# Attention and a squared-ReLU feed-forward on one core: q's difference and normalisation on VectorE, a square that reads PSUM, and other half steps for the attention units

## The chip, the cores and the metric

The kernel runs on one core of a Trainium2 chip. The metric is the device time of the execution in microseconds (us). Its engines are TensorE (PE in the profile; its weight loads PEld), VectorE (DVE), ScalarE (ACT), GpSimd (POOL) and SyncE (SP), which here issues nearly all DMAs. Matmul results go to banks of PSUM; everything else lies in SBUF.

## The reference

```python
def _attn_ref(q, k, v):                       # 8 batches, 8 heads, 576 rows, 64 columns
    q_s = np.exp(q - np.max(q, axis=-1, keepdims=True))
    q_s = q_s / (np.sum(q_s, axis=-1, keepdims=True) + 1e-09)
    k_s = np.exp(k - np.max(k, axis=2, keepdims=True))
    k_s = k_s / (np.sum(k_s, axis=2, keepdims=True) + 1e-09)
    kv = np.einsum('bhsd,bhse->bhde', k_s, v)
    return np.einsum('bhsd,bhde->bhse', q_s, kv)

def _moe_ref(x, w_in, w_out):                 # 4608 tokens, 512 -> 2048 -> 512
    r = np.maximum(x @ w_in, 0.0)
    return (r * r) @ w_out
```

The attention is linear: q is normalised along its 64 columns, k along its rows, and the result of all heads of a batch, 576 tokens of 512 columns, is the input x of the feed-forward part.

## The kernel before

**Blocks, steps and half steps.** A batch gives a block of 512 tokens; the 64 tokens left over of each batch are put by in DRAM (`x_left`) and make a ninth block at the end. For a block, the 2048 hidden columns are worked in 16 chunks, and one chunk is one step. Step n does on PE the hidden products H(n) (`ffn_h`: 12 matmuls of 128x512, L350 to L352) and then the output products of the step two before, O(n-2) (`ffn_out`: 12 matmuls, L379 to L381). Every float32 product is split into a high and a low part in PE's rounded format, so that three matmuls (high x high, high x low, low x high) replace one.

**Around a step.** ScalarE takes the relu of the bank (L356), VectorE squares it (L357), ScalarE casts the square to g_hi (L362), and VectorE subtracts to get g_lo (L367), which stands ahead of the next step's square in VectorE's queue. H writes two banks in turn, so H(n+2) writes the bank of H(n). g_hi and g_lo have two buffers each, so the cast of step n needs O(n-2) to be done with its buffer.

**Units in half steps.** While block b runs through the feed-forward part, the attention of block b+1 is prepared beside it. Heads go in pairs (two heads lie on the 128 partitions of one product), and two pairs make a couple, the first and the second pair; a block has two couples, the first couple and the second couple. The steady part has 24 pairs, numbered from 0, in 12 couples. Each pair's work is cut into units, small functions that issue a few instructions, and `UNIT_AT` gives for each unit the half step, relative to the couple's base, in which it is issued: the first number for the first pair, the second for the second pair. Half step 2n lies between H(n) with its square and O(n-2); half step 2n+1 lies behind O(n-2) and the cast to g_hi of step n. The bases are half steps 6 and 20 of a block's 32 (`COUPLE_AT`). The whole order is written by hand in this way: each engine works its instructions in the order of issue, and waits are by semaphore. What is issued in one half step follows the number of the pair and then the order of names in `UNIT_AT`.

**The units.** For k: `k_max` reduces over the rows that a partition holds, `k_bound` makes from that one bound for all rows (two transposes of 32x32 blocks, small copies and reductions, L228 to L241), `k_less` subtracts it (L246), `k_exp` is ScalarE's exponential (L249). For q: `q_max` (L253), `q_less`, the difference (L258, GpSimd), `q_exp` (L261), `q_sum` (L265, and a small addition on GpSimd, L266), `q_recip` (L269), `q_norm`, the product with the reciprocal (L273, GpSimd), `q_turn`, a transpose in blocks (L277), `q_out` and `q_back`, which write the result to DRAM and load it back turned (L283, L288) into the one tile qT. `q_split` splits qT into a high part (ScalarE, L301) and a low part (GpSimd, L302) for each head, in the tiles qs.

**The products.** At the couple's base, `kv` does the key-value products of both pairs (L338) and VectorE scales them to kf. `parts` splits kf into the one tile kvs (ScalarE L211 and L294, VectorE L212). `low` and `high` are the attention products: 320 columns and 256 columns for each of the two heads (L311), into the two banks that the attention has. Each is emptied by two copies on ScalarE (L313) and two additions on VectorE (L314); then ScalarE casts x_hi (L318) and GpSimd subtracts to get x_lo (L319). Since both write the same two banks, high must wait until the additions of low have read them. `low` also writes the left-over tokens to `x_left`.

**Loads.** `load_after` issues the loads for the pair two further on: q behind `q_less`, the first pair's k behind `k_less`, the second pair's k and all v one half step behind the couple's products `kv`. All go through SP's queue, in order, as do q's way through DRAM and the output's stores.

**The first phase** (blocks 0 and 1 of attention, all weights, and the feed-forward part of block 0) follows a list of its own, `FIRST`, and ends at about 134 us. Its square (L602) reads the relu's result and the bank.

Of the kernel before, what the change touches and what calls it, by code (L numbers as in the profile page):

```python
# [14 lines left out]
ALU = mybir.AluOpType  # L15
AX = mybir.AxisListType

P = 128
HALF = 64
LOW = 5  # L20
# [14 lines left out]


UNIT_AT = dict(
    k_max=(-13, -5), k_bound=(-11, -3), k_less=(-9, -2), k_exp=(-9, -1), q_max=(-13, -6), q_less=(-12, -6),
    q_exp=(-11, -5), q_sum=(-10, -4), q_recip=(-9, -3), q_norm=(-9, -3), q_turn=(-7, -1), q_out=(-7, -1),
    q_back=(-6, 1), q_split=(-2, 5), parts=(0, 5), low=(3, 7), high=(4, 8),  # L40
)


# [50 lines left out]
def attention_ffn_kernel(ctx: ExitStack, tc: tile.TileContext, q, k, v, w_in, w_out, out):  # L94
    nc = tc.nc

    B, H, S, D = q.shape
# [95 lines left out]
    def tiles(b, pr):  # L193
        i = pr if b == 0 else pr % NB
        return kt[i], qt[i], (v0 if b == 0 else vt)[i]

    def load_one(b, pr, n):
        for part in range(4 if n == 2 and b else 2):
            load_part(b, pr, n, part)
# [14 lines left out]
    def attention(b, pr):  # L214

        kk, qq, vv = tiles(b, pr)
        st = {}
# [8 lines left out]
        def k_bound():  # L226
            mt = attn_pool.tile([P, 4, BLK], F32, name="mt", bufs=1)
            nc.vector.transpose(mt, st["m"].rearrange("p h (e a) -> p (h e) a", a=BLK))  # L228
            m1 = attn_pool.tile([P, 4], F32, name="m1", bufs=1)
            nc.vector.tensor_reduce(m1, mt, axis=AX.X, op=ALU.max)  # L230
            m4 = attn_pool.tile([BLK, 4, 4], F32, name="m4", bufs=1)
            for g in range(4):
                nc.vector.tensor_copy(m4[:, g], m1[g * BLK : (g + 1) * BLK])
            m5 = attn_pool.tile([P, 4, 1], F32, name="m5", bufs=1)
            for g in range(4):
                nc.vector.tensor_reduce(
                    m5[g * BLK : (g + 1) * BLK, :, 0], m4.rearrange("p g c -> p c g"), axis=AX.X, op=ALU.max
                )
            mb = attn_pool.tile([P, 2, 1, D], F32, name="mb", bufs=1)
            nc.vector.tensor_copy(mt, m5.broadcast_to([P, 4, BLK]))  # L240
            nc.vector.transpose(mb.rearrange("p h o (e a) -> p (h o e) a", a=BLK), mt)  # L241
            st["mb"] = mb
# [12 lines left out]
        def q_less():  # L255
            qn = st["qn"] = attn_pool.tile([P, LOW, 2, D], F32, name="qn", tag="qn", bufs=1)
            qm = st["qm"].broadcast_to([P, 2, LOW, D])
            nc.gpsimd.tensor_tensor(qn.rearrange("p j h d -> p h j d"), qq, qm, op=ALU.subtract)  # L258

        def q_exp():  # L260
            nc.scalar.activation(st["qn"], st["qn"], AF.Exp)  # L261
# [1 line left out]
        def q_sum():  # L263
            qs = st["qs"] = attn_pool.tile([P, LOW * 2, 1], F32, name="qs")
            nc.vector.tensor_reduce(qs, st["qn"].rearrange("p j h d -> p (j h) d"), axis=AX.X, op=ALU.add)  # L265
            nc.gpsimd.tensor_scalar_add(qs, qs, 1e-9)  # L266

        def q_recip():
            nc.vector.reciprocal(st["qs"], st["qs"])  # L269

        def q_norm():
            qv = st["qn"].rearrange("p j h d -> p (j h) d")
            nc.gpsimd.tensor_tensor(qv, qv, st["qs"].broadcast_to([P, LOW * 2, D]), op=ALU.mult)  # L273

        def q_turn():
            tb = st["tb"] = w_pool.tile([P, 4, LOW, BLK], F32, name="tb", tag="raw", bufs=RAWB)
# [28 lines left out]
        def attn(g0, nj):  # L305
            xf = w_pool.tile([P, 2, 2, nj, BLK], F32, name="xf", tag="raw", bufs=RAWB)
            x, corr = xf[:, 0], xf[:, 1]
            ps = [bank(2 * nj * BLK).rearrange("p (g j a) -> p g j a", g=2, a=BLK) for h in range(2)]
            for h in range(2):
                qs = st["q"][h][:, g0 : g0 + 2, :nj].rearrange("p g j a -> p g (j a)")  # L310
                nc.tensor.matmul(ps[h].rearrange("p g j a -> p g (j a)"), kvs[:, h], qs, start=True, stop=True)  # L311
            for h in range(2):
                nc.scalar.copy(corr[half[h]], ps[h][HALF:])  # L313
                nc.vector.tensor_tensor(x[half[h]], ps[h][:HALF], corr[half[h]], op=ALU.add)  # L314
            xh, xl = (
                t[b % 2][:, pr].rearrange("p (j g a) -> p g j a", g=4, a=BLK)[:, g0 : g0 + 2] for t in (x_hi, x_lo)
            )
            nc.scalar.copy(xh, x[:, :, :HIGH])  # L318
            nc.gpsimd.tensor_tensor(xl, x[:, :, :HIGH], xh.bitcast(F32), op=ALU.subtract)  # L319
            if nj == LOW:  # L320
                dst = x_left[:, pr, b * LEFT : (b + 1) * LEFT].rearrange("p (g a) -> p g a", g=2)
                nc.sync.dma_start(dst, x[:, :, HIGH])

        st["v"] = vv
        st["units"] = dict(
            k_max=k_max, k_bound=k_bound, k_less=k_less, k_exp=k_exp, q_max=q_max, q_less=q_less, q_exp=q_exp,
            q_sum=q_sum, q_recip=q_recip, q_norm=q_norm, q_turn=q_turn, q_out=q_out, q_back=q_back, q_split=q_split,
            parts=parts, low=lambda: attn(0, LOW), high=lambda: attn(2, HIGH),
        )
        return st  # L330
# [23 lines left out]
    def relu_square(ps):  # L354
        r = work.tile([P, NT], F32, name="r")
        nc.scalar.activation(r, ps, AF.Relu)  # L356
        nc.vector.tensor_tensor(r, r, r, op=ALU.mult)  # L357
        return r

    def high_part(r):  # L360
# [9 lines left out]
    def ffn_h(blk, fc):  # L370
        ps = next_bank("h")
        for cc in range(NCC):
            h_part(ps, blk, fc, cc)
        return ps
# [256 lines left out]
    def open_late():  # L631
# [3 lines left out]
        x_lo.append(late.tile([P, NCC, NT], F32R, name="x_lo1"))  # L635

    steady = [attention(2 + i // NPAIR, i % NPAIR) for i in range((B - 2) * NPAIR)]
    with tc.manual_schedule():
        first_phase()
# [8 lines left out]
    def at(slot, *units):  # L648
        slots.setdefault(slot, []).extend(units)

    def load_after(i, n):
        if i + NB < len(steady):
            load_one(2 + (i + NB) // NPAIR, (i + NB) % NPAIR, n)

    for i, st in enumerate(steady):
        base = 2 * NFC * (1 + i // NPAIR) + COUPLE_AT[i % NPAIR // 2]
        if i % 2 == 0:
            at(base, lambda i=i: kv(steady[i : i + 2]))
        for name, when in UNIT_AT.items():
            if i or name in ("q_split", "parts", "low", "high"):  # L660
                at(base + when[i % 2], st["units"][name])
            if i and name == "q_less":
                at(base + when[i % 2], lambda i=i: load_after(i, 1))
            elif i and name == "k_less" and i % 2 == 0:
                at(base + when[0], lambda i=i: load_after(i, 0))
        if i % 2:
            for j, part in (i, 0), (i - 1, 2), (i, 2):
                at(base + 1, lambda j=j, part=part: load_after(j, part))
# [8 lines left out]
    with tc.manual_schedule():  # L677
        for n in range(NFC, len(steps) + LAG):
            if n < len(steps):
                h = ffn_h(*steps[n])  # L680
                if mid:
                    gs[n - 1] = low_part(*mid)
                r = relu_square(h)
# [45 lines left out]
```

## Time and profile before

| | us |
|---|---|
| median of 3 runs | 910.36 (907.1 to 910.5) |
| the profiled execution | 907.09 |
| its span, first to last instruction | 905.1 |
| mean granted TensorE clock | 0.991 |

| engine | busy, us | share of the span |
|---|---|---|
| PE | 867.1 | 96% |
| VectorE | 579.4 | 64% |
| ScalarE | 407.6 | 45% |
| GpSimd | 280.7 | 31% |

A row of the profile's timeline gives the start, the duration, the engine, the line, the operation, the tile written and the tiles read, the shape, and in brackets the idle time ahead of it with what ended it. A row that ends in x2 or x4 merges instructions that follow each other. Matmuls are pipelined: a matmul of 512 columns is shown with 0.39 us, but back to back one starts every 0.227 us. A group's row gives its busy time in us and the mean of one in ns.

### The profile page before, as it was taken

The numbers are of one execution on the slowest core, as the hardware profiler recorded it, in microseconds if no ns is written. First come the engines' busy times: TensorE is split into PE (matmuls) and PEld (weight loads), VectorE is DVE, ScalarE is ACT, GpSimd is POOL, SyncE is SP. The second block draws the span as 40 slices with busy tenths as digits, with TensorE's granted clock in tenths as the row PEclk, the third lists the DMA queues.
The fourth block names the chain that finished last, engine by engine and source line by source line (L and its number), as shares of the span: only waits on it lengthen the run. The fifth ranks groups of instructions, "written<-read, shape, count | busy, mean of one in ns | idle before, by whom it ended". The sixth has DMA issues, their size and how long they took to land.

```text
span 905.1 us, 12692 instructions
## 1 busy us (share of the span) xinstructions
PE 867.1 (96%) x4391; PEld 706.2 (78%) x4391; DVE 579.4 (64%) x1075; ACT 407.6 (45%) x793; POOL 280.7 (31%) x261
## 2 busy tenths in 40 slices
PE   7999998899999999899989999899989999999998
PEld 7787777787887878787878788787878888888886
DVE  7897768767778578757867687857776433223222
ACT  5997653544444444444453544443453432222222
POOL 4695723323334223333333333422342200000000
PEclk8999999999999999999999999999999999999999
DMA  9999633230332224121323133222411030002001
GB/s 239 302 312 251 161 78 85 67 91 22 102 83 72 56 80 120 57 72 42 104 69 89 39 102 83 58 70 59 120 37 34 3 93 1 1 1 47 0 1 47
DMA packets 99552, 75.82 MB, mean 84 GB/s; under 512 B 49056, under 2 KB 88736, under 8 KB 99488
## 3 DMA queue, kind: packets, MB, share of 16 engines
q1 hardware_dynamic: 98832, 74.32, 30.5%
q10 hardware_dynamic: 656, 0.69, 0.3%
q8 instruction: 35, 0.57, 0.3%
q14 instruction: 29, 0.24, 0.1%
HBM read 55.31 MB, written 19.66 MB: 83 GB/s over the span
## 4 chain that ended last, share of the span: by engine, by line
PE 71%; DVE 13%; ACT 5%; DMA 4%; SPq 3%; issue 3%; POOL 0%; ACTq 0%; DVEq 0%; POOLq 0%
PE o_ps L379 12%; PE o_ps L380 11%; PE o_ps L381 11%; PE bank L350 10%; PE bank L352 10%; PE bank L351 10%; DVE kvs L212 2%; DVE xf L314 2%; DVE r L357 2%; ACT qs L301 2%; PE bank L338 1%; DMA bounce<-tb 1%; PE bank L311 1%; DMA vt<-in_v_dram 1%; ACT g_hi L362 1%
## 5 line engine op out<-in xcount | busy, mean ns | idle before, releaser
L379 PE MATMUL o_ps<-wo,g_hi 128*128 128x512 f32 x576 | 228.7, 397 | 0.0
L380 PE MATMUL o_ps<-wo,g_hi 128*128 128x512 f32 x576 | 226.3, 393 | 0.2 <-POOL wo L585 0.2
L381 PE MATMUL o_ps<-wo,g_lo 128*128 128x512 f32 x576 | 226.2, 393 | 0.1
L350 PE MATMUL bank<-x_hi,wi 128*128 128x512 f32 x568 | 222.1, 391 | 0.0
L352 PE MATMUL bank<-x_hi,wi 128*128 128x512 f32 x568 | 221.6, 390 | 0.4 <-POOL wi L585 0.3
L351 PE MATMUL bank<-x_lo,wi 128*128 128x512 f32 x568 | 221.3, 390 | 0.0
L357 DVE TENSOR_TENSOR r<-r 128x512 f32<-128x512 f32 x128 | 107.7, 841 | 137.7 <-ACT r L356 137.6
L362 ACT CAST g_hi<-r 128x512 fp32r<-128x512 f32 x128 | 79.5, 621 | 156.2 <-PE o_ps L380 108.4
L356 ACT ACTIVATE r<-bank 128x512 f32<-128x512 f32 x128 | 76.3, 596 | 159.1 <-PE bank L352 158.2
L367 DVE TENSOR_TENSOR g_lo<-r,g_hi 128x512 fp32r<-128x512 f32 x128 | 98.5, 770 | 62.7 <-ACT g_hi L362 62.4
L381 PEld LDWEIGHTS o_ps<-wo,g_lo 128*128 128x128 f32 x576 | 109.2, 190 | 23.8 <-DVE g_lo L608 0.4
L380 PEld LDWEIGHTS o_ps<-wo,g_hi 128*128 128x128 f32 x576 | 109.5, 190 | 22.3 <-POOL wo L585 0.8
L379 PEld LDWEIGHTS o_ps<-wo,g_hi 128*128 128x128 f32 x576 | 109.5, 190 | 22.2
L352 PEld LDWEIGHTS bank<-x_hi,wi 128*128 128x128 f32 x568 | 106.7, 188 | 23.7 <-POOL wi L585 1.2
L351 PEld LDWEIGHTS bank<-x_lo,wi 128*128 128x128 f32 x568 | 106.7, 188 | 21.4 <-DVE x_lo L550 0.2
L350 PEld LDWEIGHTS bank<-x_hi,wi 128*128 128x128 f32 x568 | 106.8, 188 | 21.1
L319 POOL TENSOR_TENSOR x_lo<-xf,x_hi 128x256 fp32r<-128x256 f32 x48 | 35.5, 739 | 209.8 <-ACT x_hi L318 209.8
L302 POOL TENSOR_TENSOR qs<-qT,qs 64x640 fp32r<-64x640 f32 x48 | 84.8, 1766 | 8.1 <-ACT qs L301 4.5
L314 DVE TENSOR_TENSOR xf<-bank,xf 64x320 f32<-64x320 f32 (+1 forms) x96 | 43.0, 448 | 42.3 <-ACT xf L313 34.1
L258 POOL TENSOR_TENSOR qn<-qt,qm 128x640 f32<-128x640 f32 x23 | 32.5, 1411 | 75.6 <-DVE qm L253 63.4
L212 DVE TENSOR_TENSOR kvs<-kf,kvs 64x64 fp32r<-64x64 f32 x48 | 33.4, 695 | 33.9 <-ACT kvs L211 32.1
L311 PE MATMUL bank<-qs,kvs 128*128 128x320 f32 (+1 forms) x96 | 26.5, 328 | 24.9 <-DVE xf L314 20.2
(161 smaller groups left out, 868.8 us busy)
## 6 DMA issues: line engine op xcount, KB each, us to landing
out_dram<-o SPq DMA_DIRECT2D x71, 128.0 KB, 2.4
bounce<-tb SPq DMA_DIRECT2D x28, 320.0 KB, 2.2
qT<-bounce SPq DMA_DIRECT2D x104, 80.0 KB, 2.0
raw_i<-in_moe_w_in_dram SPq DMA_DIRECT2D x16, 512.0 KB, 8.0
raw_o<-in_moe_w_out_dram SPq DMA_DIRECT2D x16, 512.0 KB, 7.8
kt<-in_k_dram SPq DMA_DIRECT2D x32, 160.0 KB, 3.0
qt<-in_q_dram SPq DMA_DIRECT2D x31, 160.0 KB, 2.9
vt<-in_v_dram SPq DMA_DIRECT2D x58, 80.0 KB, 2.6
```

Source lines behind the costliest of these rows:

```text
L302: nc.gpsimd.tensor_tensor(qs[other], qT[own], qs[own].bitcast(F32), op=ALU.subtract)
L314: nc.vector.tensor_tensor(x[half[h]], ps[h][:HALF], corr[half[h]], op=ALU.add)
L350: nc.tensor.matmul(ps, wi[fc][:, 0, sl], xh[:, cc, :], start=(cc == 0), stop=False)
L351: nc.tensor.matmul(ps, wi[fc][:, 0, sl], xl[:, cc, :], start=False, stop=False)
L352: nc.tensor.matmul(ps, wi[fc][:, 1, sl], xh[:, cc, :], start=False, stop=(cc == NCC - 1))
L356: nc.scalar.activation(r, ps, AF.Relu)
L357: nc.vector.tensor_tensor(r, r, r, op=ALU.mult)
L362: nc.scalar.copy(g_hi, r)
L367: nc.vector.tensor_tensor(g_lo, r, g_hi.bitcast(F32), op=ALU.subtract)
L379: nc.tensor.matmul(acc, g_hi[:, ts], wo[fc][:, 0], start=(n == 0), stop=False)
L380: nc.tensor.matmul(acc, g_hi[:, ts], wo[fc][:, 1], start=False, stop=False)
L381: return nc.tensor.matmul(acc, g_lo[:, ts], wo[fc][:, 0], start=False, stop=(n == NFC - 1))
```

## The change

The diff changes five things.

1. `UNIT_AT` has other half steps. The second pair's low and high go from 7 and 8 to 8 and 10, the first pair's from 3 and 4 to 3 and 5. The split of the first pair's q goes from -2 to 1, q's way back from -6 and 1 to -3 and 3. In the dictionary `parts`, `low` and `high` now stand first, and `q_split` behind them, so that in a half step which has them all, the products and the parts are issued ahead of the split.
2. The bound of k is cut in two, `k_bound` and `k_spread`, one half step apart. `q_recip` goes into `q_sum`.
3. `NINTH_AT` gives half steps of its own to pair 1, the second pair of the very first couple; these are the first units of the steady part.
4. `q_less`, `q_norm` and the small addition in `q_sum` go from GpSimd to VectorE.
5. The square in `relu_square` multiplies the relu's result by the bank, instead of the result by itself.

```diff
 UNIT_AT = dict(
-    k_max=(-13, -5), k_bound=(-11, -3), k_less=(-9, -2), k_exp=(-9, -1), q_max=(-13, -6), q_less=(-12, -6),
-    q_exp=(-11, -5), q_sum=(-10, -4), q_recip=(-9, -3), q_norm=(-9, -3), q_turn=(-7, -1), q_out=(-7, -1),
-    q_back=(-6, 1), q_split=(-2, 5), parts=(0, 5), low=(3, 7), high=(4, 8),
+    parts=(0, 5), low=(3, 8), high=(5, 10), k_less=(-7, -1), k_exp=(-6, -1), q_split=(1, 5), k_max=(-13, -8),
+    k_bound=(-11, -3), k_spread=(-10, -2), q_max=(-12, -7), q_less=(-12, -5), q_exp=(-11, -4), q_sum=(-9, -3),
+    q_norm=(-6, -2), q_turn=(-5, -1), q_out=(-5, -1), q_back=(-3, 3),
+)
+NINTH_AT = dict(
+    k_max=-6, k_bound=-5, k_spread=-4, k_less=-3, k_exp=-2, q_max=-5, q_less=-4, q_exp=-3, q_sum=-2, q_norm=-1, q_turn=0,
+    q_out=0,
 )
...
+            st["mt"], st["m4"] = mt, m4
+
+        def k_spread():
+            mt, m4 = st["mt"], st["m4"]
             m5 = attn_pool.tile([P, 4, 1], F32, name="m5", bufs=1)
...
-            nc.gpsimd.tensor_tensor(qn.rearrange("p j h d -> p h j d"), qq, qm, op=ALU.subtract)
+            nc.vector.tensor_tensor(qn.rearrange("p j h d -> p h j d"), qq, qm, op=ALU.subtract)
...
-            nc.gpsimd.tensor_scalar_add(qs, qs, 1e-9)
-
-        def q_recip():
-            nc.vector.reciprocal(st["qs"], st["qs"])
+            nc.vector.tensor_scalar_add(qs, qs, 1e-9)
+            nc.vector.reciprocal(qs, qs)
...
-            nc.gpsimd.tensor_tensor(qv, qv, st["qs"].broadcast_to([P, LOW * 2, D]), op=ALU.mult)
+            nc.vector.tensor_tensor(qv, qv, st["qs"].broadcast_to([P, LOW * 2, D]), op=ALU.mult)
...
-    nc.vector.tensor_tensor(r, r, r, op=ALU.mult)
+    nc.vector.tensor_tensor(r, r, ps, op=ALU.mult)
...
-                at(base + when[i % 2], st["units"][name])
+                at(base + (NINTH_AT.get(name, when[1]) if i == 1 else when[i % 2]), st["units"][name])
             if i and name == "q_less":
-                at(base + when[i % 2], lambda i=i: load_after(i, 1))
+                at(base + when[i % 2] + (i == 1), lambda i=i: load_after(i, 1))
```

Line numbers of the changed kernel are higher by 4 to 8. The rows below show what stands in an engine's queue in one second couple (pairs 10 and 11), from the second pair's products on; names are the tiles of the kernel, written from read.

VectorE before, from the second pair's parts (kvs) to its low product's additions (xf):

```order
L212 TENSOR_TENSOR kvs<-kf,kvs 64x64 x2
L224 TENSOR_REDUCE m<-kt_79 128x128
L253 TENSOR_REDUCE qm<-qt_83 128x10
L367 TENSOR_TENSOR g_lo<-r,g_hi 128x512
L357 TENSOR_TENSOR r<-r 128x512
L314 TENSOR_TENSOR xf<-bank_89,xf 64x320
L314 TENSOR_TENSOR xf<-bank_90,xf 64x320
```

VectorE now, the same stretch:

```order
L216 TENSOR_TENSOR kvs<-kf,kvs 64x64 x2
L228 TENSOR_REDUCE m<-kt_79 128x128
L373 TENSOR_TENSOR g_lo<-r,g_hi 128x512
L363 TENSOR_TENSOR r<-r,bank_88 128x512
L261 TENSOR_REDUCE qm<-qt_83 128x10
L266 TENSOR_TENSOR qn<-qt_83,qm 128x2x5x64
L232 STREAM_TRANSPOSE mt<-m 128x128
L234 TENSOR_REDUCE m_4036<-mt 128x4
L237 COPY m_4038<-m_4036 32x4 x4
L373 TENSOR_TENSOR g_lo<-r,g_hi 128x512
L363 TENSOR_TENSOR r<-r,bank_87 128x512
L320 TENSOR_TENSOR xf<-bank_89,xf 64x320
```

Between the parts and the low product's additions stand one more step's g_lo and square, q's difference (L266), and the first part of the next pair's bound.

ScalarE before, from a relu to the copies of the second pair's high product:

```order
L356 ACTIVATE r<-bank_88 128x512
L362 CAST g_hi<-r 128x512
L313 COPY xf<-bank_89 64x320
L313 COPY xf<-bank_90 64x320
L318 CAST x_hi_91<-xf 128x2x4x32
L261 ACTIVATE qn<-qn 128x640
L356 ACTIVATE r<-bank_87 128x512
L313 COPY xf<-bank_89 64x256
L313 COPY xf<-bank_90 64x256
```

ScalarE now:

```order
L362 ACTIVATE r<-bank_88 128x512
L368 CAST g_hi<-r 128x512
L269 ACTIVATE qn<-qn 128x640
L362 ACTIVATE r<-bank_87 128x512
L319 COPY xf<-bank_89 64x320
L319 COPY xf<-bank_90 64x320
L324 CAST x_hi_91<-xf 128x2x4x32
L368 CAST g_hi<-r 128x512
L362 ACTIVATE r<-bank_88 128x512
L319 COPY xf<-bank_89 64x256
L319 COPY xf<-bank_90 64x256
```

The copies of the low product stand behind a relu instead of a g_hi cast, q's exponential stands ahead of them, and a g_hi cast and a relu lie between low's and high's copies.

GpSimd before, from the second pair's split to the next couple's key-value products (the memset of kt):

```order
L302 TENSOR_TENSOR qs_3983<-qT,qs_3983 64x640
L302 TENSOR_TENSOR qs_3986<-qT,qs_3986 64x640
L258 TENSOR_TENSOR qn<-qt_83,qm 128x2x5x64
L319 TENSOR_TENSOR x_lo_92<-xf,x_hi_91 128x2x4x32 x2
L266 TENSOR_SCALAR qs<-qs 128x10
L273 TENSOR_TENSOR qn<-qn,qs 128x640
L258 TENSOR_TENSOR qn<-qt_84,qm 128x2x5x64
L266 TENSOR_SCALAR qs<-qs 128x10
L273 TENSOR_TENSOR qn<-qn,qs 128x640
L302 TENSOR_TENSOR qs_4277<-qT,qs_4277 64x640
L302 TENSOR_TENSOR qs_4280<-qT,qs_4280 64x640
L345 MEMSET kt_80 64x2x64
```

GpSimd now:

```order
L308 TENSOR_TENSOR qs_3989<-qT,qs_3989 64x640
L308 TENSOR_TENSOR qs_3992<-qT,qs_3992 64x640
L325 TENSOR_TENSOR x_lo_92<-xf,x_hi_91 128x2x4x32 x2
L351 MEMSET kt_80 64x2x64
L308 TENSOR_TENSOR qs_4366<-qT,qs_4366 64x640
L308 TENSOR_TENSOR qs_4369<-qT,qs_4369 64x640
```

GpSimd keeps the splits, the x_lo subtractions and the memset; the next first pair's split comes behind the memset instead of ahead of it.

More of the change, by code (lines that the diff above doesn't have):

```diff
@@ L325, in attention @@
         st["units"] = dict(
-            k_max=k_max, k_bound=k_bound, k_less=k_less, k_exp=k_exp, q_max=q_max, q_less=q_less, q_exp=q_exp,
-            q_sum=q_sum, q_recip=q_recip, q_norm=q_norm, q_turn=q_turn, q_out=q_out, q_back=q_back, q_split=q_split,
+            k_max=k_max, k_bound=k_bound, k_spread=k_spread, k_less=k_less, k_exp=k_exp, q_max=q_max, q_less=q_less, q_exp=q_exp,
+            q_sum=q_sum, q_norm=q_norm, q_turn=q_turn, q_out=q_out, q_back=q_back, q_split=q_split,
             parts=parts, low=lambda: attn(0, LOW), high=lambda: attn(2, HIGH),
```

## The prediction

> **What bounds the kernel now.** I read the page's shares first, then a table by stage, then the matmuls one by one. All times below are microseconds unless marked ns.
>
> ```profile
> span 905.1 us, 12692 instructions
> PE 867.1 (96%) x4391; PEld 706.2 (78%) x4391; DVE 579.4 (64%) x1075; ACT 407.6 (45%) x793; POOL 280.7 (31%) x261
> ```
>
> TensorE (PE) is busy 96% of the span, so only its idle or slow time can be won. The next view gives busy time by stretch (PE, weight loads, VectorE = DVE, ScalarE = ACT, GpSimd = POOL) and then the granted clock.
>
> ```profile
> 219.40:222.80 3.40, 3.40 (x9) 2.65 (x9) 3.15 (x14) 2.15 (x5) 0.74 (x1) 0.51 0.06 10
> 390.00:490.00 100.00, 95.49 (x482) 77.81 (x481) 72.39 (x140) 44.82 (x91) 33.77 (x31) 0.98 0.27 74
> 740.00:790.00 50.00, 50.00 (x222) 41.45 (x221) 15.46 (x23) 13.89 (x24) 0.00 (x0) 1.00 0.02 8
> ```
>
> After 740, with no attention left, PE never idles. In the steady part it idles 4.51 of 100, and in one 3.4 stretch it ran at half clock. The chain that ended last shows the rhythm: here the key-value products of the second couple of successive blocks.
>
> ```profile
> 390.61 1.32 PE bank L338 x40
> ...
> 490.51 1.32 PE bank L338 x40
> ...
> 588.83 1.32 PE bank L338 x40
> ```
>
> A block lasts 99.90 or 98.32; the longer one holds a half-clock spell, worth 1.58. Now the matmuls around the second pair's products (L311), first in a first couple:
>
> ```profile
> 467.66 0.31 PE L311 MATMUL bank<-qs,kvs 128*128 128x320 f32 x1
> 468.51 0.39 PE L311 MATMUL bank<-qs,kvs 128*128 128x320 f32 x1 [0.55 <-DVE kvs L212]
> 468.74 0.39 PE L350 MATMUL bank<-x_hi,wi 128*128 128x512 f32 x1
> ...
> 471.24 0.39 PE L352 MATMUL bank<-x_hi,wi 128*128 128x512 f32 x1
> 473.28 0.91 PE L311 MATMUL bank<-qs,kvs 128*128 128x256 f32 x2 [1.65 <-DVE xf L314]
> 474.02 0.39 PE L379 MATMUL o_ps<-wo,g_hi 128*128 128x512 f32 x1
> ```
>
> then in a second couple:
>
> ```profile
> 313.34 0.46 PE L311 MATMUL bank<-qs,kvs 128*128 128x320 f32 x2
> 313.64 0.39 PE L350 MATMUL bank<-x_hi,wi 128*128 128x512 f32 x1
> ...
> 316.16 0.39 PE L352 MATMUL bank<-x_hi,wi 128*128 128x512 f32 x1
> 318.60 0.90 PE L311 MATMUL bank<-qs,kvs 128*128 128x256 f32 x2 [2.05 <-DVE xf L314]
> 319.34 0.39 PE L379 MATMUL o_ps<-wo,g_hi 128*128 128x512 f32 x1
> ```
>
> A first pair runs without a wait:
>
> ```profile
> 403.19 0.40 PE L311 MATMUL bank<-qs,kvs 128*128 128x256 f32 x2
> 403.43 0.39 PE L379 MATMUL o_ps<-wo,g_hi 128*128 128x512 f32 x1
> ...
> 406.20 0.39 PE L350 MATMUL bank<-x_hi,wi 128*128 128x512 f32 x1
> ```
>
> A clean low product takes 0.30 (313.34 to 313.64), a clean high one 0.24 (403.19 to 403.43), a half step 2.72 (468.74 to 471.24, and one matmul of 0.227). So a first couple loses 1.08 - 0.30 = 0.78 at low and 474.02 - 471.24 - 0.23 - 0.24 = 2.31 at high: **3.1**. A second couple loses 319.34 - 316.16 - 0.23 - 0.24 = **2.7** at high. One wait more stands at the steady part's start, where the first couple's second keys come late:
>
> ```profile
> PE bank L338 <- ACT kt L249: 2.4, 1, 2.4
> ```
>
> **Why they wait.** In a second couple, shortly after the half step that ends at 406.20:
>
> ```profile
> 406.69 1.47 ACT L301 CAST qs<-qT 64x640 fp32r<-64x640 f32 x2
> ...
> 415.26 0.62 ACT L362 CAST g_hi<-r 128x512 fp32r<-128x512 f32 x1 [5.40 <-DVE r L357]
> 415.90 0.86 ACT L313 COPY xf<-bank 64x320 f32<-64x320 f32 x2
> ```
>
> ```profile
> 407.55 3.20 POOL L302 TENSOR_TENSOR qs<-qT,qs 64x640 fp32r<-64x640 f32 x2 [0.75 <-ACT qs L301]
> 413.06 1.57 POOL L258 TENSOR_TENSOR qn<-qt,qm 128x640 f32<-128x640 f32 x1 [2.30 <-DVE qm L253]
> ```
>
> ```profile
> 408.47 2.37 DVE L212 TENSOR_TENSOR kvs<-kf,kvs 64x64 fp32r<-64x64 f32 x2 [2.92 <-ACT kvs L211]
> ...
> 413.42 1.75 DVE L357 TENSOR_TENSOR r<-r 128x512 f32<-128x512 f32 x1
> ```
>
> GpSimd's split runs, VectorE's kvs subtraction takes 2.37 beside it, the reductions queue behind that, the square takes 1.75 beside GpSimd's q difference, ScalarE's g_hi idles 5.40 for it, and the copies of the low product stand behind g_hi on ScalarE. High needs the two banks those copies empty. The square's price is bounded by two rows, the old one (with itself twice) in the steady part, and the first phase's, which already reads the bank:
>
> ```profile
> L357 DVE TENSOR_TENSOR r<-r 128x512 f32<-128x512 f32 x81 | 73.2, 904 | 54.4 <-ACT r L356 54.4
> ```
>
> ```profile
> L602 DVE TENSOR_TENSOR r<-r,bank 128x512 f32<-128x512 f32 x5 | 3.4, 674 | 0.5 <-ACT r L599 0.5
> ```
>
> **The change part by part.**
>
> *Low and high two half steps apart.* From low to high, old waits included, passed 318.60 - 313.34 = 5.26 and 473.28 - 467.66 = 5.62. The new distance without a wait is 0.30 + 2 x 2.72 = 5.74. So both old high waits fit even if nothing else improved. Besides, the second pair's low moves to an even half step, where its copies follow the relu and no longer g_hi, with its 5.40. Gain: 2.31 or 2.7 a couple.
>
> *The second pair's split and low.* Low comes three half steps behind the split (before: two), but ScalarE first does high's copies and cast for the first pair and the parts. Counted from the end of the output half step: g_hi 0.5 (406.20 to 406.69); two copies, the wait for VectorE's addition and the cast, an estimate of 1.9 from copies of 0.86 (415.90), two additions and a cast of 0.6; four small casts, some 1.1; then 0.86 to the first GpSimd split (406.69 to 407.55) and 3.20 for both: 7.6. PE arrives after 0.24 + 3 x 2.72 = 8.4. Margin 0.8; the wait is bounded by 0 and, from the old low, 0.78. I take 0. The kvs subtractions now stand ahead of the split and no longer start beside it.
>
> *The first pair's split and low.* This split moves from half step -2 to +1, two before low. It begins 0.5 behind the half step's end: 0.5 + 0.86 + 3.20 = 4.6 against 5.44. Margin 0.9; again 0, and at most 0.78.
>
> *q's difference and normalisation, the small addition, on VectorE.* The nearest rows are the key difference, same shape, free of GpSimd and beside it:
>
> ```profile
> 468.40 0.83 DVE L246 TENSOR_TENSOR ke<-kt,mb 128x640 f32<-128x640 f32 x1
> ```
>
> ```profile
> 444.05 2.20 DVE L246 TENSOR_TENSOR kt<-kt,mb 128x640 f32<-128x640 f32 x1
> ```
>
> I take 0.83, since GpSimd keeps only the splits and x_lo; the addition is some 0.1. Per block VectorE gains 4 x (2 x 0.83 + 0.1) = 7.0 and loses 16 x (0.904 - 0.674) = 3.7 on squares: 72.4 of 100 becomes some 75 of 92, PE's work covers it. At 2.20 it would be 4 x 2 x 1.37 = 11 more, still 86 of 92.
>
> *The square reads the bank.* The bank is now held until the square, not the relu. Its next writer begins three half steps, 8.2, after the bank was full. By the order and these durations the worst square, behind the second pair's split, ends some 4 after; 4 are left. Cost 0.
>
> *The key chain ahead of the key-value products.* VectorE's queue in the last three half steps is fullest where output stores fall. From
>
> ```profile
> 439.12 0.30 DVE L228 STREAM_TRANSPOSE mt<-m 128x128 f32<-128x128 f32 x1
> ...
> 441.50 0.31 DVE L241 STREAM_TRANSPOSE mb<-mt 128x128 f32<-128x128 f32 x1
> 441.83 0.63 DVE L367 TENSOR_TENSOR g_lo<-r,g_hi 128x512 fp32r<-128x512 f32 x1
> ```
>
> bound and spread take 2.7 together; q's sum with addition and reciprocal some 1.1; g_lo 0.63, square 0.67, normalisation and key difference 1.66. From 439.12 that is 445.9, and ScalarE's exponential of the same 640 columns, some 0.75, ends at 446.6. PE started the couple there at 446.6 and needs the second keys half of the 1.32 later. Margin 0.6, cost 0. In the first couple of all everything is a half step earlier, so its 2.4 goes.
>
> *Queues passed.* qT's load for the second pair goes behind the ten key and value loads, and x_left, on SP:
>
> ```profile
> 392.37 1.74 SPq L288 DMA_DIRECT2D qT<-bounce  x4
> ...
> 402.25 0.39 SPq L322 DMA_DIRECT2D x_left<-xf  x1
> ```
>
> From 402.6, with 1.74 of issue and about 2.0 to land, it is there at 406.4; the split's casts, 406.69 before, now start near 409.7. Hidden by 3; without that cover each late microsecond goes to low.
>
> **The sum.** Six first couples 6 x 3.1 = 18.6; five second couples 5 x 2.7 = 13.5 (the last, with no next block's preparation beside it, never waited); the start 2.4; three half-clock spells 3 x 1.58 = 4.7, all beside these waits. Together 39.2. The profiled execution took 907.1 (span 905.1 and 2.0 around it): 907.1 - 39.2 = **868**. The runs' median, 910.4, is 3.3 above it, about two more spells of 1.58; without waits I expect none of them, so 868 stands for the median too.
>
> The Trainium skill bears on the 4.7: "TensorE: Matmul & The Clock Gate", Part 1: The HAM clock gate, has the clock halved only after an idle window of about 3.4. Here waits of 1.7 to 2.1 stand beside the slow spell (0.51), so the measurement decides; by that rule the spells have another cause and stay.
>
> **The rivals.**
>
> 1. *A split comes late at low.* For it: margins of only 0.8 and 0.9, and GpSimd's split can be held up by VectorE. Against: VectorE has little beside it there. 11 couples with 0.78 twice: 17 back, 885; for one of the two sites, 877.
> 2. *The half-clock spells stay* though the waits go: 868 + 4.7 = 873. For it, the waits are short; against, no spell stands after 740, where PE does not wait.
> 3. *The change does half of what it says*: ScalarE's q exponential, ahead of the low copies, now waits for VectorE's q difference, and high still waits half of 2.31 or 2.7: 868 + 14 = 882 with no spells, 887 with them.
> 4. *Slower: the key chain is late.* VectorE's queue ahead of each couple; it decides from a backlog of 0.6, and the sign turns where the wait passes 39.2 / 12 = 3.3, a backlog of 3.9. Three operations with two inputs in SBUF (q difference, normalisation, key difference), each at 2.20 for 0.83, give 4.1: 12 x 3.5 = 42, with 0.5 of restart each (0.74 - 0.24 at 473.28) 6 more, and the three spells: 868 + 53 = 921. Against: GpSimd has no split in those half steps.
>
> The Trainium skill speaks against the move here: "SBUF — State Buffer", Who interferes with whom, says that a VectorE instruction with two SBUF inputs and a GpSimd one that reads SBUF exclude each other for a whole instruction, whichever comes first. The trace agrees (0.83 and 2.20). Where no split runs, that rule and my sum give the same; at the splits it would give rival 1 or 4.
>
> **How the numbers follow.** Forecast 0.62, within 864 to 872; rival 1 0.16; rival 2 0.08; rival 3 0.09; rival 4 0.03; 0.02 for something unseen that leaves the time. A measurement here can tell about 0.5% from no change. The range 863 to 886 takes in the forecast, rival 2, rival 1 and part of rival 3, and a third of a per cent below. Faster 0.95, same 0.02, slower 0.03.
>
> **What would show it.** Right: PE busy nearly 100 of 100 in the steady part, clock 1.00, blocks of 92.5 (98.32 - 3.1 - 2.7), no L311 wait for xf, squares near 0.68, key differences near 0.83, GpSimd under half as busy. Wrong: an idle time at low put down to qs (rival 1), spells without waits (2), xf waits at high (3), the second keys waited for at every couple (4). I am wrong by more than the range if VectorE's queue, not PE, sets the block.

## The result, and the profile after

| | before | changed |
|---|---|---|
| median of 4 runs, us | 910.43 (907.1 to 911.6) | 867.17 (865.14 to 870.45) |
| the profiled execution, us | 907.09 | 865.14 |
| its span, us | 905.1 | 863.4 |
| mean granted clock | 0.991 | 0.997 |

The ratio is 0.9534, with a 95% interval of 0.9492 to 0.9576. Forecast were 868 and a range of 863 to 886.

The changed kernel's page gives busy time and share of the span for each engine, and the granted clock in tenths by slices of the span:

```profile
span 863.4 us, 12640 instructions
PE 853.9 (99%) x4391; PEld 701.9 (81%) x4391; DVE 577.0 (67%) x1144; ACT 404.5 (47%) x793; POOL 198.8 (23%) x192
...
PEclk9999999999999999999999999999999999999999
```

Busy time by stretch in the changed kernel (PE, weight loads, VectorE, ScalarE, GpSimd, then the granted clock), in the same steady stretch as before:

```profile
390.00:490.00 100.00, 100.00 (x515) 82.76 (x514) 78.94 (x169) 47.84 (x97) 21.90 (x21) 1.00 0.29 78
```

PE is busy 100 of 100 where it was 95.49. The chain that ended last in the changed kernel, at the key-value products of second couples:

```profile
369.12 1.32 PE bank L344 x40
...
461.67 1.32 PE bank L344 x40
...
554.21 1.32 PE bank L344 x40
```

Every block lasts 92.55 (before 98.3, or 99.9 with a half-clock spell). From the first couple's key-value products to the end the profiled execution took 759.4 before (from 145.74) and now 720.2 (from 143.12): **39.2 less, the sum of the prediction**. The other 2.6 of the span's 41.8 lie ahead of that, in the first phase, which the diff does not touch; in the twelve other profiles below those products begin anywhere from 143.2 to 148.9.

One second couple of the changed kernel, engine by engine, from its second pair's split on. PE first (L317 are the attention products):

```profile
300.32 0.46 PE L317 MATMUL bank<-qs,kvs 128*128 128x320 f32 x2
...
306.08 0.40 PE L317 MATMUL bank<-qs,kvs 128*128 128x256 f32 x2
306.32 0.39 PE L385 MATMUL o_ps<-wo,g_hi 128*128 128x512 f32 x1
```

GpSimd and ScalarE:

```profile
296.02 3.56 POOL L308 TENSOR_TENSOR qs<-qT,qs 64x640 fp32r<-64x640 f32 x2 [1.00 <-ACT qs L307]
```

```profile
298.83 0.62 ACT L368 CAST g_hi<-r 128x512 fp32r<-128x512 f32 x1 [1.56 <-DVE r L363]
...
301.61 0.87 ACT L319 COPY xf<-bank 64x320 f32<-64x320 f32 x2
```

VectorE:

```profile
294.38 0.97 DVE L216 TENSOR_TENSOR kvs<-kf,kvs 64x64 fp32r<-64x64 f32 x2 [0.62 <-ACT kvs L215]
...
296.62 1.52 DVE L373 TENSOR_TENSOR g_lo<-r,g_hi 128x512 fp32r<-128x512 f32 x1
298.07 0.67 DVE L363 TENSOR_TENSOR r<-r,bank 128x512 f32<-128x512 f32 x1
...
299.50 0.82 DVE L266 TENSOR_TENSOR qn<-qt,qm 128x640 f32<-128x640 f32 x1
...
302.82 0.99 DVE L320 TENSOR_TENSOR xf<-bank,xf 64x320 f32<-64x320 f32 x2
```

The kvs subtractions end before the split begins (0.97 for both, 2.37 before); in this couple g_lo is the one operation held up by it (1.52); the square takes 0.67 beside it (1.75 before, beside GpSimd's q difference); g_hi idles 1.56 for the square (5.40 before). The split ends at 299.58, and low begins at 300.32: 0.74 to spare. The banks of low are empty at 303.81, and high begins at 306.08: 2.3 to spare. No L317 has a wait.

In first couples the second pair's split holds up two operations, g_lo and the small addition that was moved to VectorE, which takes 0.17 elsewhere:

```profile
255.46 1.38 DVE L274 TENSOR_SCALAR qs<-qs 128x10 f32<-128x10 f32 x1
...
257.01 1.99 DVE L373 TENSOR_TENSOR g_lo<-r,g_hi 128x512 fp32r<-128x512 f32 x1
```

There the banks of low are empty only 0.8 to 0.9 before high begins (0.5 in the last first couple).

### The profile page after: what moved, and what is told of

Same layout as the page of the kernel before. It is cut to its first block, busy times and chain, and to the rows that moved or that the text cites. A ratio compares the mean times of both kernels' runs of the same rounds, so it can differ in the third digit from the quotient of the medians.

```text
span 863.4 us, 12640 instructions
## 1 busy us (share of the span) xinstructions
PE 853.9 (99%) x4391; PEld 701.9 (81%) x4391; DVE 577.0 (67%) x1144; ACT 404.5 (47%) x793; POOL 198.8 (23%) x192
## 4 chain that ended last, share of the span: by engine, by line
PE 88%; DMA 4%; ACT 3%; DVE 3%; SPq 1%; issue 1%; POOL 0%; ACTq 0%; DVEq 0%; POOLq 0%
PE o_ps L385 14%; PE o_ps L386 14%; PE o_ps L387 14%; PE bank L356 14%; PE bank L358 14%; PE bank L357 13%; PE bank L344 2%; DMA kt<-in_k_dram 2%; PE bank L317 1%; DMA bounce<-tb 1%; DVE bank L577 1%; DMA raw_o<-in_moe_w_out_dram 1%; ACT bank L574 1%; DVE w L582 1%; PE early L626 1%
## 5 line engine op out<-in xcount | busy, mean ns | idle before, releaser
L363 DVE TENSOR_TENSOR r<-r,bank 128x512 f32<-128x512 f32 x128 | 87.4, 683 | 124.1 <-ACT r L362 123.8
L362 ACT ACTIVATE r<-bank 128x512 f32<-128x512 f32 x128 | 76.5, 598 | 148.9 <-PE bank L358 148.4
L385 PEld LDWEIGHTS o_ps<-wo,g_hi 128*128 128x128 f32 x576 | 108.3, 188 | 22.0
L386 PEld LDWEIGHTS o_ps<-wo,g_hi 128*128 128x128 f32 x576 | 108.2, 188 | 22.0 <-POOL wo L591 0.8
L308 POOL TENSOR_TENSOR qs<-qT,qs 64x640 fp32r<-64x640 f32 x48 | 77.3, 1610 | 58.5 <-ACT qs L307 45.5
L324 ACT CAST x_hi<-xf 128x256 fp32r<-128x256 f32 x48 | 19.5, 407 | 53.7 <-DVE xf L320 53.7
L351 POOL MEMSET kt<- 64x128 f32 x12 | 2.4, 201 | 166.2 <-PE bank L344 166.2
L319 ACT COPY xf<-bank 64x320 f32<-64x320 f32 (+1 forms) x96 | 38.0, 396 | 2.3
```

Of the source, the lines that this page charges most:

```text
L308: nc.gpsimd.tensor_tensor(qs[other], qT[own], qs[own].bitcast(F32), op=ALU.subtract)
L363: nc.vector.tensor_tensor(r, r, ps, op=ALU.mult)
L385: nc.tensor.matmul(acc, g_hi[:, ts], wo[fc][:, 0], start=(n == 0), stop=False)
L386: nc.tensor.matmul(acc, g_hi[:, ts], wo[fc][:, 1], start=False, stop=False)
```

## The experiments

Twelve kernels, in four groups, each with runs of the kernel before beside it, whose medians were 909.2 to 911.6. In the tables of waits a row names the engine, the tile and line that waited, what it waited for, the total in us, the times and the longest. "Block" is the distance of a block's key-value products to the next block's in the profile, without half-clock spells.

**1. The spacing alone.** The kernel before, with low and high two half steps apart.

```diff
-    q_back=(-6, 1), q_split=(-2, 5), parts=(0, 5), low=(3, 7), high=(4, 8),
+    q_back=(-6, 1), q_split=(-2, 5), parts=(0, 5), low=(3, 8), high=(5, 10),
```

> The kernel before with one edit: low and high at half steps (3, 8) and (5, 10) instead of (3, 7) and (4, 8). The theory of the prediction is that low and high are 0.30 + 2 x 2.72 = 5.74 us apart without a wait, where 5.26 and 5.62 passed with the waits included, so that both high waits (2.31 and 2.7) and the wait at low (0.78) go with this alone and the half-clock spells with them; the late second keys at the start (2.4) stay: about 907 - 36.8 = 870 to 874. The rival is that the waits come from VectorE being held up by GpSimd (the kvs subtraction 2.37, the square 1.75): then VectorE is as late as before, the wait moves on to low and to the next step, and 890 to 905 are left.

Measured: 895.64, ratio 0.9833 (0.9786 to 0.9879), block 96.9. PE's waits in its profile:

```profile
PE bank L338 <- ACT kt L249: 9.9, 7, 2.4
PE bank L311 <- DVE xf L314: 3.0, 5, 0.6
PE bank L350 <- ACT x_hi L318: 2.9, 5, 0.6
...
PE bank L351 <- POOL x_lo L319: 1.6, 5, 0.3
```

and ScalarE behind the second pair's split:

```profile
414.23 0.62 ACT L362 CAST g_hi<-r 128x512 fp32r<-128x512 f32 x1 [5.52 <-DVE r L357]
```

The time is in the rival's range. In first couples the waits at low and high are gone. In second couples VectorE is as late as before (g_hi idles 5.52): a part of the wait at high stays (0.6), and a part goes to the next block's first hidden products, which now follow the last high by fewer half steps. Besides, the second keys of second couples now come late (some 1.25 each). VectorE ahead of one of them:

```profile
378.83 0.86 DVE L314 TENSOR_TENSOR xf<-bank,xf 64x256 f32<-64x256 f32 x2
...
383.73 1.75 DVE L357 TENSOR_TENSOR r<-r 128x512 f32<-128x512 f32 x1
385.40 2.18 DVE L246 TENSOR_TENSOR kt<-kt,mb 128x640 f32<-128x640 f32 x1
```

The additions of the first couple's high, two half steps later than before, stand right ahead of the key chain, whose square and key difference run beside GpSimd's normalisation and split.

**2. The square alone.** The kernel before, with the square reading the bank.

```diff
-        nc.vector.tensor_tensor(r, r, r, op=ALU.mult)
+        nc.vector.tensor_tensor(r, r, ps, op=ALU.mult)
```

> The kernel before with one edit: the square multiplies the relu by the bank. Both theories expect squares of 0.68 us instead of a mean of 0.90. In second couples the square beside GpSimd's q difference (1.75) ends 1.07 earlier, so the high wait there falls from 2.2 to about 1.1; in first couples the square lost only 0.2: 5 x 1.07 + 6 x 0.2 = 6.6, so about 900 to 904. If the bank's later release mattered, PE would wait ahead of the hidden products (L350) and the time would be above 910.

Measured: 899.61, ratio 0.9876 (0.9828 to 0.9924), block 97.0. Squares and PE's waits at high:

```profile
L357 DVE TENSOR_TENSOR r<-r,bank 128x512 f32<-128x512 f32 x82 | 56.1, 684 | 81.5 <-ACT r L356 81.5
```

```profile
PE bank L311 <- DVE xf L314: 13.5, 11, 1.4
```

The time is 0.4 below the range, and its parts are as expected: 684 ns instead of 904, 13.5 at high instead of 20.2, and no wait ahead of L350.

**3. The engines alone.** The kernel before, with its half steps, but q's difference, normalisation and small addition on VectorE, and the square reading the bank.

```diff
-            nc.gpsimd.tensor_tensor(qn.rearrange("p j h d -> p h j d"), qq, qm, op=ALU.subtract)
+            nc.vector.tensor_tensor(qn.rearrange("p j h d -> p h j d"), qq, qm, op=ALU.subtract)
...
-            nc.gpsimd.tensor_tensor(qv, qv, st["qs"].broadcast_to([P, LOW * 2, D]), op=ALU.mult)
+            nc.vector.tensor_tensor(qv, qv, st["qs"].broadcast_to([P, LOW * 2, D]), op=ALU.mult)
...
```

> The kernel before with its half steps, but q's difference, normalisation and small addition on VectorE and the square reading the bank. The theory of the prediction: the kvs subtraction still starts beside the split (2.37) and high still follows low by one half step, so most of the waits stay; VectorE has 0.83 more ahead of the first couples' square and the second couples gain as with the square alone: 897 to 908. The rival (the hold-ups by GpSimd are what costs): more than half of the 39 goes, 885 or less.

Measured: 907.43, ratio 0.9963 (0.9933 to 0.9992), block 97.9. Within what was expected. Beside run 2 (block 97.0), moving q's work to VectorE costs time under the old half steps.

**4. The half steps alone.** The changed kernel, with q's work on GpSimd and the square of the relu with itself, as before (the edits of 3 and 2, the other way).

> The changed kernel's half steps, but q's difference, normalisation and small addition on GpSimd and the square of the relu with itself, as before. The theory of the prediction: the products are two half steps apart, so the waits at high are gone; the normalisation on GpSimd (1.5) stands beside the key difference in the last half steps ahead of the key-value products, which then takes 2.2 instead of 0.83, against a margin of 0.6: a wait of about 0.8 in 12 couples with some restart, 868 + 10 to 15 = 878 to 883. The rival (the engines carry the gain): the waits at high stay, 890 to 905.

Measured: 890.47, ratio 0.9771 (0.972 to 0.9822), block 95.35. Neither theory: the time is in the rival's range, but no wait at high is left. All of it stands at the second keys of second couples, 6 waits of some 2.4:

```profile
PE bank L344 <- ACT kt L257: 14.8, 6, 2.7
```

VectorE ahead of one of them, where high of the couple before and the key chain fall together:

```profile
274.25 0.84 DVE L283 STREAM_TRANSPOSE tb<-qn 128x640 f32<-128x640 f32 x1 [2.51 <-POOL qn L279]
...
275.59 1.75 DVE L363 TENSOR_TENSOR r<-r 128x512 f32<-128x512 f32 x1
...
281.82 1.75 DVE L363 TENSOR_TENSOR r<-r 128x512 f32<-128x512 f32 x1
```

VectorE stands 2.51 for GpSimd's normalisation, and two squares take 1.75 beside GpSimd. I had looked for the price at the key difference, which takes 0.83 there. The profiled execution took 886.4 at a mean clock of 0.995, with one half-clock spell; the three other runs show 0.987 to 0.989, so the median seems to hold more spells than this profile.

**5 to 8. One part taken back from the changed kernel.** The square (5), q's work (6), the distance of high (7), and the order of names, so that in a half step the split is issued ahead of the parts (8):

```diff
-    nc.vector.tensor_tensor(r, r, ps, op=ALU.mult)
+    nc.vector.tensor_tensor(r, r, r, op=ALU.mult)
```

> The changed kernel with one edit taken back: the square multiplies the relu by itself. The theory: with q's work on VectorE, only the splits and x_lo are left on GpSimd, so only the squares beside a split (one a pair at most) wait, for at most one split of 1.57; the queue has 0.7 at the late split and 2.1 at high to give, so PE waits little: blocks of 92.6 to 93.2, 867 to 871. The rival, that the bank-reading square is what takes the hold-ups away: blocks of 94 or more, 876 or later.

Measured: 868.51, ratio 0.9544 (0.95 to 0.9589), block 92.67. Squares are slow again, and PE does not wait for them:

```profile
L363 DVE TENSOR_TENSOR r<-r 128x512 f32<-128x512 f32 x86 | 74.4, 865 | 46.7 <-ACT r L362 46.5
```

> The changed kernel with q's difference, normalisation and small addition back on GpSimd; the square still reads the bank. In the run with only the new half steps the key-value products of second couples waited 2.4 for the second keys; there VectorE had waited 2.5 for GpSimd's normalisation ahead of q's transpose, and two squares of 1.75 instead of 0.68 stood ahead of the key difference. The theory that both add up in one queue: with squares of 0.68 the wait falls by 2 x 1.07 to about 0.3, with restart 0.8 a block: blocks of 93.0 to 93.8, 871 to 876. The rival, that the wait for the normalisation alone sets it: blocks near 95.3 as before, 886 to 890.

Measured: 872.01, ratio 0.959 (0.9544 to 0.9636), block 93.07; the wait at the second keys falls as the queue's sum says, from 2.4 to 0.3:

```profile
PE bank L344 <- ACT kt L257: 1.6, 6, 0.5
```

```diff
-    parts=(0, 5), low=(3, 8), high=(5, 10), k_less=(-7, -1), k_exp=(-6, -1), q_split=(1, 5),
+    parts=(0, 5), low=(3, 8), high=(4, 9), k_less=(-7, -1), k_exp=(-6, -1), q_split=(1, 5),
```

> The changed kernel with high one half step behind low: low=(3, 8), high=(4, 9). In the changed kernel the additions that empty low's banks end 3.5 after low begins on PE (300.32 to 303.81); high would come 0.30 + 2.72 = 3.02 after it. The theory: a wait of about 0.5 with 0.5 of restart at second pairs (22 or fewer waits of the pairs have margin at first pairs), 11 x 1.0 = 11: about 878, no more, since VectorE is no longer late. The rival, that the distance is the whole of the gain: the old waits of 2.3 and 2.7 come back, 895 or later.

Measured: 871.38, ratio 0.9583 (0.9537 to 0.9629), block 93.28. Less than expected: only first couples' high waits, some 0.25, and its second matmul 0.5 more, since it writes the second bank, whose addition ends that much later (263.58 to 264.10 in one couple, against 0.12 without a wait).

```diff
-    parts=(0, 5), low=(3, 8), high=(5, 10), k_less=(-7, -1), k_exp=(-6, -1), q_split=(1, 5),
+    k_less=(-7, -1), k_exp=(-6, -1), q_split=(1, 5), parts=(0, 5), low=(3, 8), high=(5, 10),
```

> The changed kernel with the old order of names in a half step: the split is issued ahead of the parts and the products. The theory: then VectorE's kvs subtractions start beside the split again and are held up by it (0.97 for both now, 2.37 before), and with them VectorE's queue, by some 1.5 to 2; margins of 0.7 at low and 2.1 at high are used up in part: 868 to 876. If issue order within the half step does not matter: 868, blocks of 92.55.

Measured: 874.0, ratio 0.9612 (0.9557 to 0.9667), block 93.6. VectorE in the half step of the second pair's split:

```profile
299.10 2.50 DVE L216 TENSOR_TENSOR kvs<-kf,kvs 64x64 fp32r<-64x64 f32 x2 [2.12 <-ACT kvs L215]
```

The subtractions take 2.50 beside the split again; the wait that follows is at the next block's x_lo, 0.3 by the profile and, by the starts of PE's matmuls, some 0.9 a block in all. By the blocks (93.6 against 92.67 to 93.28) the order of names is thus worth more than any other single part of 5 to 8; in time it lies 2.0 behind the nearest, with intervals that overlap.

**9 and 10. The rest of the table, and the cut of the bound.** 9 is the kernel of 3 with the spacing of 1, so the changed kernel with all other half steps, the bound and the order of names as before; 10 is the changed kernel with the bound in one half step.

> The changed kernel with all half steps and the order of names as before, but for low and high, which keep (3, 8) and (5, 10); q's work on VectorE and the square reading the bank as changed. With the spacing alone, blocks of 96.9 had waits of 1.25 at the second keys, 0.75 at high and 1.3 at the next block's first hidden products. The theory that VectorE's queue behind the products is what counts: squares of 0.68 and no GpSimd ahead of q's exponential take the last two away, and a wait of 0.4 to 1.2 at the second keys stays, since the split at half step -2 still stands beside the key difference: blocks of 93.0 to 94.2, 870 to 880. The rival, that the other moved units carry as much as the engines: blocks of 95 or more, 884 or later.

Measured: 904.1, ratio 0.9928 (0.9896 to 0.996), block 98.25: the rival, and worse than it said. PE's waits:

```profile
PE bank L338 <- ACT kt L249: 15.1, 12, 3.0
PE o_ps L381 <- DVE g_lo L367: 3.0, 6, 0.5
```

GpSimd and VectorE ahead of the key-value products:

```profile
385.15 3.68 POOL L302 TENSOR_TENSOR qs<-qT,qs 64x640 fp32r<-64x640 f32 x2 [2.49 <-ACT qs L301]
```

```profile
385.42 1.97 DVE L273 TENSOR_TENSOR qn<-qn,qs 128x640 f32<-128x640 f32 x1
387.32 2.06 DVE L367 TENSOR_TENSOR g_lo<-r,g_hi 128x512 fp32r<-128x512 f32 x1
...
389.89 0.81 DVE L246 TENSOR_TENSOR kt<-kt,mb 128x640 f32<-128x640 f32 x1
```

With the first pair's split at half step -2, the normalisation and g_lo, both with two inputs in SBUF, each stand until the half of it that is under way has ended (1.97 and 2.06, against 0.83 and 0.68 away from it), and the key difference is late.

> The changed kernel with the two halves of the key bound in one half step again (k_spread at the half step of k_bound). Both halves together are 2.7 on VectorE. The theory: the low product's copies and the square behind them have 2.1 to give at high, so an added 1.3 in that half step costs nothing or a short wait: blocks of 92.5 to 93.2, 867 to 872. The rival, that cutting the bound is needed to keep the square in time: a wait of 1 or more at high in each couple, blocks of 95 or more.

Measured: 871.7, ratio 0.9583 (0.9544 to 0.9621), block 93.07. The cut is worth 0.5 a block; the time lost is again at the second keys (0.3 each), not at high.

**11 and 12. The cause within the table.** Kernel 9 with only the split moved, then with the order of names besides:

```diff
-    q_back=(-6, 1), q_split=(-2, 5), parts=(0, 5), low=(3, 8), high=(5, 10),
+    q_back=(-6, 3), q_split=(1, 5), parts=(0, 5), low=(3, 8), high=(5, 10),
```

> The kernel of the run with the engines and the spacing but the old half steps, with one thing more from the changed kernel: the first pair's split at half step 1 instead of -2 (and the second pair's q way back at 3 instead of 1, as it must follow). There, ahead of the key-value products, the normalisation took 1.97 and g_lo 2.06 beside the split, and the second keys came 1.64 late in second couples, 0.44 in first, 2.98 at the start. The theory: the place of the split, now that q's work is on VectorE, is what the old half steps cost there; these waits go (0 to 0.2 left) with their restart, and the waits behind the second pair's split stay (0.66 at g_lo; 0.4 at high; 0.49 and 0.58 at the next block): blocks of 94.8 to 96.0 instead of 98.25, 881 to 890. The rival, that the key chain's own half steps do it: the second keys stay late by 1 or more, blocks of 97 or more.

Measured: 883.79, ratio 0.9726 (0.9699 to 0.9754), block 95.53. The waits at the second keys are gone, but for one of 1.0 in the first couple of all, and the others stand as forecast:

```profile
PE o_ps L381 <- DVE g_lo L367: 3.1, 6, 0.5
...
PE bank L351 <- POOL x_lo L319: 1.5, 5, 0.3
PE bank L350 <- ACT x_hi L318: 1.5, 5, 0.3
PE bank L311 <- DVE xf L314: 1.2, 5, 0.3
```

```diff
-    k_max=(-13, -5), k_bound=(-11, -3), k_less=(-9, -2), k_exp=(-9, -1), q_max=(-13, -6), q_less=(-12, -6),
+    parts=(0, 5), low=(3, 8), high=(5, 10), k_max=(-13, -5), k_bound=(-11, -3), k_less=(-9, -2), k_exp=(-9, -1), q_max=(-13, -6), q_less=(-12, -6),
...
-    q_back=(-6, 3), q_split=(1, 5), parts=(0, 5), low=(3, 8), high=(5, 10),
+    q_back=(-6, 3), q_split=(1, 5),
```

> The same with the order of names of the changed kernel: parts, low and high ahead of the split in a half step. The theory: the kvs subtractions then end ahead of the split (2.48 for both beside it) and VectorE's queue behind them is 1.5 to 2 earlier, which takes the waits at g_lo, at high and at the next block: blocks of 92.6 to 93.6, 868 to 876, though all other half steps are the old ones. The rival, that the rest of the table (q's sum, normalisation and turn later, the bound cut in two, the second pair's maxima earlier) carries a part of its own: blocks of 94 or more, 877 or later.

Measured: 871.97, ratio 0.9593 (0.9569 to 0.9618), block 92.97. In the steady part PE's only wait named is the first couple's:

```profile
PE bank L338 <- ACT kt L249: 1.0, 1, 1.0
```

So five edits of the change (the spacing, the split's half step, the order of names, q's work on VectorE, the square) bring the block from 98.3 to 92.97. The rest of the change (the other half steps, the cut bound, pair 1's own half steps) gives the last 0.4 and takes away the wait at the start.

| kernel | block, us | median, us |
|---|---|---|
| before | 98.3 | 910.43 |
| spacing (1) | 96.9 | 895.64 |
| q's work and square (3) | 97.9 | 907.43 |
| spacing, q's work, square (9) | 98.25 | 904.1 |
| the same and the split moved (11) | 95.5 | 883.79 |
| the same and the parts first (12) | 92.97 | 871.97 |
| all half steps, no engine moved (4) | 95.35 | 890.47 |
| changed, without spacing / parts first / cut bound | 93.28 / 93.6 / 93.07 | 871.38 / 874.0 / 871.7 |
| changed, without square / q's work | 92.67 / 93.07 | 868.51 / 872.01 |
| changed | 92.55 | 867.17 |

No version here is faster than the changed kernel. Run 5, with the old square, is 1.3 behind it with overlapping ranges, so at the end the square is worth 0.12 a block by the profiles and nothing that the times can tell.

## Why the prediction was right, and where its reasons were not

**The sum** was right: 39.2 in the steady part, all waits at low and high, the wait at the start and the half-clock spells gone, and blocks of 92.55 where 92.5 stood. But it adds up PE's waits as the old trace has them and comes out for any change that removes them all without a new one; that it came out does not test the reasons given for each part.

**The margins** were right to a few tenths. Second pair's split: 0.8 forecast, 0.74 measured (299.58 to 300.32). Within it two errors offset each other: the split takes 3.56 instead of 3.20, held up beside g_lo, and starts 0.2 earlier than worked out. First pair's split: 0.9 forecast, 0.9 measured. The key chain: 0.6 forecast; the second keys' exponential and PE's need of them:

```profile
275.93 0.74 ACT L257 ACTIVATE kt<-kt 128x640 f32<-128x640 f32 x1 [1.64 <-DVE kt L254]
```

```profile
277.13 0.75 PE L344 MATMUL bank<-vt,kt 128*64 128x65 f32 x20
```

276.67 to 277.13, 0.46 (some 0.8 in the steady first couples, and under 0.1 in the last couple of all). q's difference was priced at 0.83 and takes 0.82; the square at 0.67 and takes 0.68.

**Sizes that were off.** The small addition, priced at 0.1, takes 1.38 in each first couple, beside the split. VectorE's busy time was to rise to 75 a block and stayed at 72 (72.3 before, 71.9 now, summed over one block's rows), since the kvs subtractions and the key differences, freed from GpSimd, take 5.9 less a block, a gain that the sum left out. "GpSimd under half as busy" failed: 19.3 a block against 33.7, as the splits and x_lo that stay are most of its work. And the slower rival's 0.5 of restart (0.74 - 0.24 at high) is in the main the second matmul's wait for the second bank's addition; at the second keys a wait costs 0.3 to 0.4 more than itself (run 10: 0.24 and 0.5 a block; run 4: 2.4 and 2.8).

**"So both old high waits fit even if nothing else improved" was wrong.** Run 1 did just that, and a block fell from 98.3 to 96.9, not to 92.5. The distance from low to high covers the wait at high in first couples; in second couples VectorE's backlog behind the split was not gone and is met at high and at the next block's input, and, by the order of the trace, the later additions of the first couple's high crowd the key chain, so that the second keys are late. I had taken a wait for a property of its place.

**The split's move was filed under costs**, as a margin of 0.9 to watch. It is what makes the move of q's work pay: with the split at -2, run 9 gives 904.1, and VectorE's normalisation and g_lo take 2.0 each beside it; with the split at 1, in run 11, 883.8. My price of 0.83 for a moved operation rested on "GpSimd keeps only the splits"; that was true, and the place of those splits decided. This is the mechanism of the slower rival, at a split that I had not looked at in its old place; run 9 shows it, at 1.6 a second couple. The rule of the Trainium skill ("SBUF — State Buffer", Who interferes with whom) that two-input operations and GpSimd's exclude each other agrees with it (1.97 for the normalisation and 2.06 for g_lo there; in the changed kernel the normalisation takes 0.78 to 0.83).

**The order of names** had one sentence (the kvs subtractions no longer start beside the split) and no term in the sum. It is worth 2.6 a block between runs 11 and 12 and 1.1 in the changed kernel.

**The square and q's move overlap.** Either alone, on the new half steps, does nearly all that both do: from 95.35 to 93.07 with the square (run 6), to 92.67 with q's work (run 5), to 92.55 with both. Both keep VectorE's queue short ahead of the second keys, and once that chain is in time, more haste is worth nothing.

**The half-clock spells** went with the waits, as forecast; the rival that they stay falls. The reading of the median's 3.3 as two more spells is borne out in part. Of 37 runs of the kernel before beside the experiments, all within 906 to 918, the 14 with a mean clock of 0.988 or less have a median of 912.4, the 16 with 0.991 or more one of 908.0; so the slower ones do run at a lower clock. But the changed kernel has no spell in the steady part of its profile, its four runs show a clock of 0.997 to 0.998, and they still spread over 5.3. Part of that can lie in the first phase, behind which the steady part's first products began at times up to 5.8 apart in the profiles; what moves it was not tested.

## What to carry to other kernels

When PE waits at one place, look for the backlog that made the other engine late, and not for room at that place alone: in run 1 room moved much of the wait to later users of the same queue. Where two engines exclude each other, list which operations stand beside the long one (here GpSimd's split) before moving more work to the other engine; the half step of the long one and its rank in the order were worth 2.7 and 2.6 a block, as much as the move itself on the new half steps, and without them the move gained nothing (run 9). And once a queue is in time, two remedies do the work of one: take parts back one by one to see which are needed.

## What the runs showed of the hardware

Half-clock spells last 3.41 us and lie a whole number of 3.41 apart (before, by the clock's records: 194.56 at full clock between two of them, 57 times 3.413). I laid that grid over the matmuls' records of the steady part in seven of the kernels and added up PE's idle time in each window. Thirteen spells came there, each right behind a window with 1.57 to 2.99 idle. No window with less than 1.57 was followed by one; of those between 1.57 and 1.89, some were and some not; all of 2.05 and more were. So a wait of about half a window can halve the clock for the next one, if it falls into one window; run 1 had no spell: of its 2.4 at the start 1.63 fell into one window, and its other waits were 1.26 or less. The Trainium skill ("TensorE: Matmul & The Clock Gate", Part 1: The HAM clock gate) speaks of an idle window; here half a window did.

Beside GpSimd, VectorE's square that multiplies the relu by itself took 0.68 to 1.75 in the steady part before; with the bank as one input it took 0.67 to 0.69 every time, in the changed kernel and in run 2. An operation with a single SBUF input was not free of GpSimd in every case: the small addition on 10 columns took 0.17, but 1.38 beside the split.
